# Dividing the activation's steps over a unit: three quarters with equal ScalarE work, and a transform step behind the copy out of X

## The chip, the core and the metric

The kernel runs on one core of a Trainium2 chip. The time is the device time of one execution in microseconds (us), from the first to the last instruction on that core. Before the change it is 2831.02 us, the median of three runs (2830.42 to 2831.22).

The engines have short names in the profile. PE is TensorE's matrix multiplication, and PEld is the loading of its stationary operand. DVE is VectorE, ACT is ScalarE and POOL is GpSimd. SP issues transfers. Each engine works through its own instructions strictly in the order in which they were written, so an instruction that waits holds up everything behind it on that engine.

## What is computed

The input x has 8 sequences of 3008 rows with 256 numbers each, in float32. A first part filters each sequence in the frequency domain; a second part is a two-layer network with an activation. Cut to what matters:

```
X = rfft(x, axis=1);  Y = X * (filt_r + 1j * filt_i);  a = irfft(Y, axis=1)
a = a.reshape(24064, 256)
h = a @ w_in                 # 24064 x 2048
out = (h - tanh(h)) @ w_out  # 24064 x 256
```

## The kernel before, in words

**The Fourier part** is three small dense transforms, with a round through device memory between each: `first` (64 points, tile pf), `middle` (47 points and back, with the filter in between; tiles pz on the way in and pe on the way out), and `last` (the return of the 64 points, tile pu). It is done for five groups of sequences. While the network works on one group, the transforms of the next are fed in between, one step at a time.

**The network part** treats up to 512 columns at a time (a "group" in the code; there are 48), and each group in four *units* U of 512 hidden features, so 192 units in all. A unit with its full width takes two by two blocks: instead of eight block products, it forms seven (a Strassen-Winograd scheme), both for w_in (function `up`) and for w_out (function `down`). GpSimd forms the sums of blocks (`combine`, lines 524 to 527).

Three generations of units are in work at once. While `up(U)` multiplies by w_in, `shrink(U-1)` applies the activation to the previous unit, and `down(U-2)` multiplies the one before that by w_out. Nothing plans this: `up` writes out by hand the order of everything, and calls the others through five small functions. `d()` and `e()` each advance `down` by one part (its matmuls, and at the end of a group the sums that follow them). `s()` advances `shrink` by one step, up to its next `yield`. `shrinks(k)` calls `s()` as often as the k-th number of the list `steps_at` says. `t(k)`, for k from 0 to 4, is a slot for the Fourier part: at most one step of `first`, `middle` or `last` is put there, if one is due, and some transfers of finished output. Its due times are spread evenly over a stretch of the kernel, so some stretches have a step in every slot, most have one in about every second slot, and the last 24 units have none but `last`.

**The four quarters of a unit.** The PSUM bank X takes four of `up`'s seven products one after the other: product 1, then 6, then 7, then 4. Between them X has to be read out: by ScalarE (`copied`, line 551: first into s1, then u2, then u3) and at last by VectorE (line 590, the third quarter of the tile h, called h2 below). The next product into X must wait for that copy, and the next unit's product 1 must wait for line 590. So X divides a unit into quarters, named here after their product: X1, X6, X7 and X4. The banks Y and Z take the other three products in between. TensorE's order before the change is: X1, Y, t(0), two products of `down`, t(1), X6, Z, two of `down`, t(2), X7, two of `down`, t(3), X4, one of `down`, t(4), Z, and then X1 of the next unit.

**The activation** works on the two halves of h (named 2 and 0 after where they begin). Each half passes ScalarE three times (arctan, line 611; square with a running sum, line 612; square with scale and bias, line 618) and VectorE twice (a product, line 617, which waits for line 612; a product with a sum, line 621, which waits for line 618). There are two buffers for y (lines 611, 612) and one for sq (line 618).

**The transform's steps** all use one PSUM buffer. A pz step has two matmuls (line 430), two ScalarE copies (lines 443, 444), a VectorE product that reads the same bank (line 445, tile uv) and two GpSimd operations (lines 446, 447). A pe step has two matmuls (line 411) and one ScalarE copy (line 414). A pf step is like a pe step. A pu step has eight short matmuls (line 511) and one copy (line 513). The next step's matmul can start only when the buffer has been read.

Of the kernel before, what the change touches and what calls it, by code (L numbers as in the profile page):

```python
# [143 lines left out]
def kernel(  # L144
# [10 lines left out]
    V, G, ACT = nc.vector, nc.gpsimd, nc.scalar  # L155
# [367 lines left out]
    def combine(b, t, shared=False):  # L523
        G.tensor_sub(t[0], b[0][1], b[0][0])  # L524
        G.tensor_sub(t[1], b[1][1], t[0])  # L525
        (V if shared else G).tensor_sub(t[2], b[1][1], b[0][1])  # L526
        G.tensor_sub(t[3], t[1], b[1][0])  # L527
# [4 lines left out]
    def up(U, d, e, s, t):  # L532

        i, u = divmod(U, 4)
        b, tu, w = uts[i]
        rhs = [b[0][0], b[1][0], b[1][1], tu[:, 3, 0:w], tu[:, 0, 0:w], tu[:, 1, 0:w],
               tu[:, 2, 0:w]]
        banks = {k: ps.tile([128, 2, 256], F32, tag=k, bufs=1, name=k) for k in "xyz"}
        X, Y, Z = (banks[k][:, :, 0:w] for k in "xyz")
        h = dn.tile([128, 4, 2, 256], F32, tag="h", bufs=3, name="h")  # L540
        hs[U] = (h, w)

        def mm(bank, q, first):
            for k in range(2):
                nc.tensor.matmul(bank[:, k], wu[:, q - 1, (2 * u + k) * 128:(2 * u + k + 1) * 128],  # L545
                                 rhs[q - 1], start=(first and k == 0), stop=True,
                                 skip_group_check=True)

        def copied(tag):
            t = dn.tile([128, 2, 256], F32, tag=tag, bufs=1, name=tag)[:, :, 0:w]  # L550
            ACT.copy(t, X)  # L551
            return t

        steps_at = ([1, 2, 0, 1, 0, 1, 1, 0] if U > 1 else [0, 0, 1, 0, 2, 0, 1, 2])

        def shrinks(at):
            for _ in range(steps_at[at]):  # L560
                s()

        mm(X, 1, True)
        mm(Y, 2, True)
        s1 = copied("s1")
        t(0)
        d()
        shrinks(0)
        V.tensor_add(h[:, 0, :, 0:w], Y, s1)  # L569
        e()  # L570
        shrinks(1)
        t(1)
        mm(X, 6, False)
        mm(Z, 5, True)
        u2 = copied("u2")
        shrinks(2)
        d()
        shrinks(3)
        e()
        t(2)  # L580
        mm(X, 7, False)
        u3 = copied("u3")
        V.tensor_add(h[:, 3, :, 0:w], Z, u3)  # L583
        shrinks(4)
        d()
        shrinks(5)
        e()
        t(3)
        mm(X, 4, False)
        V.tensor_copy(h[:, 2, :, 0:w], X)  # L590
        shrinks(6)
        d()
        e()
        t(4)
        mm(Z, 3, False)
        V.tensor_add(h[:, 1, :, 0:w], Z, u2)
        shrinks(7)

    def shrink(U):

        h, w = hs.pop(U)
        ht = {k: h[:, k:k + 2].rearrange("p a b n -> p (a b) n")[:, :, 0:w] for k in (0, 2)}

        def tiles(tag, bufs):
            return dn.tile([128, 4, 256], F32, tag=tag, bufs=bufs, name=tag)[:, :, 0:w]

        y, sq = {}, {}

        def start(k):
            y[k] = tiles("y", 2)  # L610
            ACT.activation(y[k], ht[k], AF.Arctan, scale=S)  # L611
            ACT.activation(y[k], y[k], AF.Square,  # L612
                           accum_out=y_sums[:, 2 * U + k // 2:2 * U + k // 2 + 1])

        def square(k):
            sq[k] = tiles("sq", 1)
            V.tensor_mul(ht[k], ht[k], y[k])  # L617
            ACT.activation(sq[k], y[k], AF.Square, bias=near_b, scale=A)  # L618

        def end(k):  # L620
            V.scalar_tensor_tensor(out=ht[k], in0=sq[k], scalar=K, in1=ht[k],  # L621
                                   op0=ALU.add, op1=ALU.mult)

        start(2)
        yield
        square(2)
        yield
        end(2)
        yield
        start(0)  # L630
        yield
        square(0)
        yield
        end(0)
        t = dn.tile([128, 4, 2, 256], F32, tag="t", bufs=2, name="t")
        blocks = [[h[:, 2 * a + k, :, 0:w] for k in range(2)] for a in range(2)]
        combine(blocks, [t[:, k, :, 0:w] for k in range(4)], U + 1 == 4 * len(groups))
        gs[U] = (blocks, t, w)
        yield
# [64 lines left out]
    def store(i, o):  # L704


        p, c = groups[i]
        r, n = CHUNKS[p][c]
        ws_ = widths(p, c)
        total = sum(ws_)  # L710
        ot = dn.tile([128, 2, CH * 128], F32, tag="ot", bufs=1, name="ot")
        for h in range(2):
            V.transpose(ot[:, h, 0:total], o[:, h, 0:total])
        b = UNITS[p][0]
        if len(UNITS[p]) == 2:
            blocks = [(r + 32 * q * NR, n, 32 * q) for q in range(4)]
        else:
            blocks = [(r_h + 32 * q * NR, n_h, rows.start + 32 * q)
                      for _, rows, r_h, n_h in halves(p, r, n) for q in range(2)]
        for h in range(2):  # L720
            for k in range(4):
                for row, m, lo in blocks:
                    outs.append((
                        dram(out.tensor, (b * SEQ + row) * DM + h * 128 + 32 * k,
                             [[NR * DM, 32], [DM, m], [1, 32]]),
                        ot[32 * k:32 * k + 32, h, :].rearrange(
                            "p (j c) -> p j c", c=128)[:, 0:m, lo:lo + 32]))
# [26 lines left out]
    def store_some(n):  # L754
        for dst, src in outs[:n]:
            nc.sync.dma_start(dst, src)
        del outs[:n]
# [81 lines left out]
    with tc.tile_pool(name="tr", bufs=2) as tr, tc.manual_schedule():  # L839
        with tc.tile_pool(name="pro", bufs=1) as pro, \  # L840
# [136 lines left out]
            for j in range(NK // 2):  # L977
# [7 lines left out]
                for i in range(2):  # L985
                    k = (2 * j + i) % 4
# [34 lines left out]
        with tc.tile_pool(name="dn", bufs=2) as dn, \  # L1021
# [40 lines left out]
            for U in range(total + 2):  # L1062
                i, u = divmod(U, 4)
                if U < total:
# [20 lines left out]
                    if u == 2 and i + 1 < len(groups):  # L1085
                        lasts = last(i + 1, z1)
                sh = shrink(U - 1) if 0 <= U - 1 < total else iter(())
                dw = down(U - 2) if 0 <= U - 2 < total else iter(())

                def d():  # L1090

                    next(dw, None)

                def e():

                    next(dw, None)

                def s():

                    next(sh, None)  # L1100

                def t(k):


                    nonlocal ms, done
                    if k == 2 and stores:
                        store(*stores.pop())
                    store_some(4)
                    if U >= total:
                        return  # L1110
                    pos = 20 * c + 5 * u + k
                    if u == 3 and k in (0, 2) and i + 1 < len(groups):
                        next(lasts)
                    elif done < len(steps) and steps[done] <= pos:
                        if done < n_f:
                            next(fs)
                        else:
                            next(ms)
                        done += 1
                        if done == n_f:  # L1120
                            ms = middle(p + 1, z1)
                            next(ms)
                    next(late, None)
                    if U > 0 and k in (1, 3):
                        next(copies, None)

                if U < total:
                    if U == total - 1:
                        one = tr.tile([128, 128], F32, tag="x", bufs=3, name="one_sb")
                        nc.sync.dma_start(one, one_d)  # L1130
                        ones = cst.tile([128, 1], F32, name="ones")
                        G.memset(ones, 1.0)
                    up(U, d, e, s, t)
                else:
                    for k in range(5):
                        s()
                        s()
                        d()
                        e()
                        t(k)  # L1140
                        if U == total + 1 and k == 0:
                            bounded(z1)
# [39 lines left out]
```

## Time and profile before

| what | before |
|---|---|
| time | 2831.02 us (2830.42 to 2831.22) |
| TensorE busy with matmuls | 2730.9 us, 96% of the span |
| VectorE busy | 1911.7 us, 68% |
| ScalarE busy | 1878.5 us, 66% |
| GpSimd busy | 1792.0 us, 63% |
| one full-width unit without a transform step | 12.09 us |
| matmul waits for the copy u2 or u3 (line 551) | 9.0 us in 24 waits |
| matmul waits for h2 (line 590) | 5.2 us in 9 waits |
| pe waits for uv (line 445) | 15.3 us in 23 waits |

The table of engines shows how long each was busy. A matmul's end is modelled, so its recorded time overlaps the next one's, and short stalls of TensorE are hidden under it. The waits of TensorE are therefore best read in two places: its matmuls (which show too little of a stall) and its weight loads (which show a little too much), and settled by the distance between the starts of two matmuls in the listing in order of time.

### The profile page before, as it was taken

To read this page: it belongs to the slowest core of one execution; us is meant where nothing else is said; L and a number is where in the kernel's file an instruction comes from. 1 tells how busy PE (TensorE), PEld (TensorE's weight loads), DVE (VectorE), ACT (ScalarE), POOL (GpSimd) and SP (SyncE) were. 2 spreads that over 40 slices of the span, in tenths; PEclk is the share of its full clock that TensorE was granted. 3 is DMA by queue.
4 is the path that set the end of the run, shared out by engine and by line. 5 is a ranking of instruction groups with operands and counts; after the bars stand their busy time and mean duration, and the time that the engine had idled before them with its cause. 6 is when DMAs were issued, how large, how long until landed. Compare 5 with 4: busy or idle time off the path is not lost.

```text
span 2831.1 us, 36652 instructions
## 1 busy us (share of the span) xinstructions
PE 2730.9 (96%) x12438; PEld 2269.8 (80%) x12438; DVE 1911.7 (68%) x2175; ACT 1878.5 (66%) x2790; POOL 1792.0 (63%) x1407
## 2 busy tenths in 40 slices
PE   4899999999999999999999999999999999999998
PEld 2577777988878777888877887788888888898887
DVE  6755556666766677666666777676676767677776
ACT  2466666666666677666677666666666676667665
POOL 5546777544777767644576777755466667655555
PEclk7999999999999999999999999999999999999999
DMA  9854443233233322222333223212222322101010
GB/s 249 217 179 118 104 116 76 71 94 85 59 81 85 77 67 54 57 81 81 85 81 74 70 66 86 49 40 68 58 65 62 79 56 53 34 18 26 16 22 17
DMA packets 322592, 217.53 MB, mean 77 GB/s; under 512 B 224782, under 2 KB 274746, under 8 KB 322156
## 3 DMA queue, kind: packets, MB, share of 16 engines
q1 hardware_dynamic: 266826, 157.28, 23.6%
q10 hardware_dynamic: 52818, 51.53, 6.0%
q0 software_dynamic: 2752, 6.30, 0.8%
q8 instruction: 100, 1.64, 0.2%
q14 instruction: 96, 0.79, 0.1%
HBM read 138.87 MB, written 79.17 MB: 77 GB/s over the span
## 4 chain that ended last, share of the span: by engine, by line
PE 78%; ACT 9%; issue 5%; DVE 5%; DMA 2%; POOL 1%; ACTq 1%; SPq 0%; DVEq 0%; POOLq 0%
PE o L663 31%; PE x L545 20%; PE z L545 9%; PE y L545 6%; PE pe L411 3%; PE pu L511 3%; ACT y L611 3%; PE pz L430 3%; PE pf L351 2%; DVE h L617 1%; ACT u L551 1%; ACT zs L444 1%; DVE uv L445 1%; ACT y L612 1%; ACT zs L443 1%
## 5 line engine op out<-in xcount | busy, mean ns | idle before, releaser
L663 PE MATMUL o<-t,wd 128*128 128x256 f32 (+2 forms) x3072 | 776.3, 375 | 1.8 <-POOL t L526 1.3
L617 DVE TENSOR_TENSOR h<-h,y 128x1024 f32<-128x1024 f32 (+2 forms) x384 | 571.3, 1488 | 275.8 <-ACT y L612 275.8
L663 PEld LDWEIGHTS o<-t,wd 128*128 128x128 f32 x3072 | 580.7, 190 | 74.2 <-POOL t L526 1.6
L545 PE MATMUL x<-tu,wu 128*128 128x256 f32 (+2 forms) x2304 | 588.0, 377 | 9.2 <-ACT u L551 9.0
L663 PE MATMUL o<-h,wd 128*128 128x256 f32 (+2 forms) x2304 | 582.5, 375 | 0.4 <-DVE h L621 0.4
L621 DVE SCALAR_TENSOR_TENSOR h<-sq,h 128x1024 f32<-128x1024 f32 (+2 forms) x384 | 568.0, 1479 | 20.6 <-ACT y L611 0.5
L524 POOL TENSOR_TENSOR t<-h 128x512 f32<-128x512 f32 (+2 forms) x192 | 240.4, 1252 | 506.8 <-DVE h L621 455.0
L545 PEld LDWEIGHTS x<-tu,wu 128*128 128x128 f32 x2304 | 427.4, 190 | 151.8 <-issue 72.6
L663 PEld LDWEIGHTS o<-h,wd 128*128 128x128 f32 x2304 | 431.1, 190 | 71.8 <-issue 18.4
L618 ACT ACTIVATE sq<-y,near_b 128x1024 f32<-128x1024 f32 (+2 forms) x384 | 435.6, 1134 | 5.0 <-DVE h L621 0.2
L611 ACT ACTIVATE y<-h 128x1024 f32<-128x1024 f32 (+2 forms) x384 | 400.0, 1042 | 15.7 <-ACT e L414 8.0
L612 ACT ACTIVATE y<-y 128x1024 f32<-128x1024 f32 (+2 forms) x384 | 399.2, 1040 | 12.2
L551 ACT COPY s<-x 128x512 f32<-128x512 f32 (+2 forms) x192 | 110.8, 577 | 441.0 <-PE x L545 432.4
L527 POOL TENSOR_TENSOR t<-t,h 128x512 f32<-128x512 f32 (+2 forms) x192 | 308.9, 1609 | 0.1
L551 ACT COPY u<-x 128x512 f32<-128x512 f32 (+2 forms) x384 | 219.2, 571 | 56.9 <-PE x L545 22.2
L583 DVE TENSOR_TENSOR h<-z,u 128x512 f32<-128x512 f32 (+2 forms) x192 | 129.5, 675 | 180.0 <-ACT u L551 177.0
L525 POOL TENSOR_TENSOR t<-h,t 128x512 f32<-128x512 f32 (+2 forms) x192 | 240.9, 1255 | 15.1
L526 POOL TENSOR_TENSOR t<-h 128x512 f32<-128x512 f32 (+2 forms) x191 | 248.0, 1298 | 0.0
L446 POOL TENSOR_TENSOR zs<-zs,ft 128x512 f32<-128x512 f32 x112 | 165.4, 1477 | 101.8 <-ACT zs L444 101.6
L447 POOL TENSOR_TENSOR uv<-uv,zs 128x512 f32<-128x512 f32 x112 | 213.7, 1908 | 15.7 <-DVE uv L445 7.2
L545 PE MATMUL x<-ut,wu 128*128 128x256 f32 (+2 forms) x768 | 199.2, 382 | 6.9 <-DVE h L590 5.2
L569 DVE TENSOR_TENSOR h<-y,s 128x512 f32<-128x512 f32 (+2 forms) x192 | 130.4, 679 | 104.9 <-PE y L545 88.6
(122 smaller groups left out, 3380.2 us busy)
## 6 DMA issues: line engine op xcount, KB each, us to landing
a<-ct SPq DMA_DIRECT2D x64, 384.0 KB, 4.1
ft<-filt SPq DMA_DIRECT2D x96, 256.0 KB, 4.6
out_dram<-ot SPq DMA_DIRECT2D x1392, 16.0 KB, 1.5
ct<-e ACTq DMA_DIRECT2D x112, 192.0 KB, 2.4
ct<-a ACTq DMA_DIRECT2D x80, 256.0 KB, 2.9
x_sb<-in_x_dram SPq DMA_DIRECT2D x69, 256.0 KB, 2.8
e<-ct SPq DMA_DIRECT2D x33, 512.0 KB, 4.7
fg<-fg SPq DMA_DIRECT2D x40, 392.0 KB, 6.0
```

Source lines behind the costliest of these rows:

```text
L524: G.tensor_sub(t[0], b[0][1], b[0][0])
L525: G.tensor_sub(t[1], b[1][1], t[0])
L526: (V if shared else G).tensor_sub(t[2], b[1][1], b[0][1])
L527: G.tensor_sub(t[3], t[1], b[1][0])
L545: nc.tensor.matmul(bank[:, k], wu[:, q - 1, (2 * u + k) * 128:(2 * u + k + 1) * 128], rhs[q - 1], start=(first and k == 0), stop=True, ski ...
L551: ACT.copy(t, X)
L611: ACT.activation(y[k], ht[k], AF.Arctan, scale=S)
L612: ACT.activation(y[k], y[k], AF.Square, accum_out=y_sums[:, 2 * U + k // 2:2 * U + k // 2 + 1])
L617: V.tensor_mul(ht[k], ht[k], y[k])
L618: ACT.activation(sq[k], y[k], AF.Square, bias=near_b, scale=A)
L621: V.scalar_tensor_tensor(out=ht[k], in0=sq[k], scalar=K, in1=ht[k], op0=ALU.add, op1=ALU.mult)
L663: nc.tensor.matmul(product(q), wd[:, q - 1, (2 * u + k) * 128: (2 * u + k + 1) * 128], rhs[q - 1][:, k], start=(u == 0 and k == 0 and q == ...
```

## The change

There are three edits.

1. The step of `shrink` that did a half's arctan and its square with sum is cut in two (`turn`, `power`), and the VectorE product is cut off from the last square (`times`, `square`). ScalarE still does the same six operations in the same order, and VectorE its four, but the `yield`s fall elsewhere. With the new list `steps_at`, ScalarE gets two of them in each of the quarters X1, X6 and X7: arctan and square with sum of half 2 in X1, the last square of half 2 and the arctan of half 0 in X6, and the square with sum and the last square of half 0 in X7. Before, it was three, two and one.
2. VectorE's line 621 for half 2 moves from X1, ahead of slot t(1), to X6, ahead of t(2).
3. The slot t(3) moves behind X4 and behind the copy out of X (line 590). Before, it stood ahead of both.

```
-        steps_at = ([1, 2, 0, 1, 0, 1, 1, 0] if U > 1 else [0, 0, 1, 0, 2, 0, 1, 2])
+        steps_at = ([1, 1, 1, 1, 0, 1, 1, 0] if U > 1 else [0, 0, 1, 0, 2, 0, 2, 1])
...
         shrinks(5)
         e()
-        t(3)
         mm(X, 4, False)
         V.tensor_copy(h[:, 2, :, 0:w], X)
+        t(3)
         shrinks(6)
...
-        def start(k):
+        def turn(k):
             y[k] = tiles("y", 2)
             ACT.activation(y[k], ht[k], AF.Arctan, scale=S)
+
+        def power(k):
             ACT.activation(y[k], y[k], AF.Square,
                            accum_out=y_sums[:, 2 * U + k // 2:2 * U + k // 2 + 1])
 
+        def times(k):
+            V.tensor_mul(ht[k], ht[k], y[k])
+
         def square(k):
             sq[k] = tiles("sq", 1)
-            V.tensor_mul(ht[k], ht[k], y[k])
             ACT.activation(sq[k], y[k], AF.Square, bias=near_b, scale=A)
...
-        start(2)
+
+        turn(2)
+        power(2)
+        yield
+        times(2)
         yield
         square(2)
+        turn(0)
         yield
         end(2)
         yield
-        start(0)
-        yield
+        power(0)
+        times(0)
         square(0)
         yield
         end(0)
```

## The prediction

> **What bounds the kernel now.** I read the page's table of engines first, then TensorE's waits, those of its weight loads, and last the listing in order of time.
>
> ```profile
> PE 2730.9 (96%) x12438; PEld 2269.8 (80%) x12438; DVE 1911.7 (68%) x2175; ACT 1878.5 (66%) x2790; POOL 1792.0 (63%) x1407
> ```
> ```profile
> 1000.00:1500.00 500.00, 496.13 (x2277) 412.35 (x2276) 334.50 (x370) 342.96 (x513) 311.02 (x236) 1.00 0.28 72
> ```
>
> TensorE is the bound, at a granted clock of 1.00; the change takes no matmul away. So it can win only TensorE's stalls, or add to them. These are the waits that the moved steps touch:
>
> ```profile
> PE pe L411 <- DVE uv L445: 15.3, 23, 2.7
> PE x L545 <- ACT u L551: 9.0, 24, 0.9
> PE x L545 <- DVE h L590: 5.2, 9, 1.8
> ```
> ```profile
> PEld x L545 <- ACT u L551: 29.2, 66, 1.1
> PEld x L545 <- DVE h L590: 22.9, 46, 2.2
> ```
>
> The columns are total us, times and longest. A recorded 256-column matmul lasts 379 ns, but in a full stretch one starts every 216 ns, so the first view hides some 0.16 us of each stall, and the second overstates. I therefore went through the listing and took the distance between starts beyond that pace: **22 us** for X6, X7 and X4, **18 us** for X1, and 42 us for pe, of which 18 are the prologue (before 123 us), untouched. That leaves 24 us of pe, nearly all in units 8 to 21, where every slot holds a step. So some 64 us are in reach.
>
> Where they arise:
>
> ```profile
> 822.07 1.13 PE L545 MATMUL x<-tu,wu 128*128 128x256 f32 x4 [0.67 <-ACT u L551]
> ```
> ```profile
> 794.20 0.69 DVE L445 TENSOR_TENSOR uv<-pz,ft 128x512 f32<-128x512 f32 x1 [1.30 <-ACT zs L444]
> 794.81 0.68 DVE L590 COPY h<-x 128x512 f32<-128x512 f32 x1
> ...
> 795.55 1.13 PE L545 MATMUL x<-ut,wu 128*128 128x256 f32 x4 [0.40 <-DVE h L590]
> ```
> ```profile
> 338.76 1.23 DVE L621 SCALAR_TENSOR_TENSOR h<-sq,h 128x1024 f32<-128x1024 f32 x1
> ...
> 339.90 0.68 DVE L445 TENSOR_TENSOR uv<-pz,ft 128x512 f32<-128x512 f32 x1
> ...
> 340.73 1.07 PE L411 MATMUL pe<-uv,fg 112*96 112x512 f32 x2 [1.54 <-DVE uv L445]
> ```
>
> First, X4 waits because u3 comes late from a busy ScalarE. Second, h2 (line 590) stands in VectorE's queue behind the uv of t(3), which waits for both ScalarE copies, and X1 waits for h2. Third, uv of t(1) stands behind line 621, and pe in t(2) waits for uv.
>
> [...] line 617 takes 937 ns at least, 1380 in the median and 2354 at most. This matters below. [...]
>
> **The change, part by part.** Times are us from the start of X1 in a full-width unit. From the listing I take these intervals: a product of `up` or `down` is 0.86 of TensorE (four matmuls of 0.216), a pz or pe step 0.87. A copy out of X can start 1.06 after its product starts; the next product into X can start 0.64 after the copy does. On ScalarE one thing follows another after 0.47 (copy), 1.09 (arctan), 1.18 (square with its sum read) and 1.06 (last square); the pair of zs copies takes 1.20 and starts at least 1.12 after pz. None of these change, since no operation does.
>
> *Relief of X6 and X7 (edit 1).* ScalarE in X1: before, s1 at 1.06, then arctan, square, last square: free at 4.86. After: 3.80. Take a unit of 820 us, with pe in t(0), pz in t(2), pe in t(4), the first of its kind in a group of four, in which `down` adds two ScalarE copies of 0.36. Before, its u3 started at 11.42 and X4 at 12.06; its slot was 11.23. After, pe's copy ends ScalarE's wait at 3.43, arctan and square take it to 5.70, p1 to 6.06, u2 to 6.55, last square and arctan to 8.70, p5 to 9.05, the zs copies to 10.26. So u3 starts at 10.26 and X4 may start at 10.90, before 11.23: the stall is gone. Where t(1) holds pz, u2 was at 7.50 and X7 waited to 8.13 for a slot of 7.77; after, u2 starts at 5.77. Moving t(3) brings X4 forward by 0.87 where t(3) has a step, but u3 then comes at 8.83 and X4 may start at 9.47, with its slot at 10.36. I take 18 of the 22 us: **−18**; between −10 (if u3 stays late where zs copies precede it) and −22.
>
> *h2 ahead of t(3) (edit 3).* h2 no longer waits for uv. Of the 18 us, 14 come from units with pz in t(3) or from unit 1, where line 621 stood in front; the rest are narrow groups and VectorE's own work. I take **−10**, between −6 and −14.
>
> *pe behind uv (edits 2 and 3).* In four dense units uv of t(1) stands no more behind line 621: 1.3 each, 2 in the last, −6. Six pe in t(3) get X4 as cover: 0.43 each, −2.6. But pz in t(3) and pe in t(4) are now one product apart (0.86) and not two (1.73), while uv comes 3 after pz: eight times +0.85, +6.8. Three pu behind uv gain 0.5 each, −1.5. Sum about **−3**, between −8 and +3.
>
> *The product of half 0 behind its square (edit 1; an added wait).* Before, line 617 of half 0 found its square long done and began as soon as h3 (line 583) was written. After, it waits for the square in X7, which starts 0.47 after u3: line 617 starts 0.47+1.18 = 1.65 after u3, and before 1.22. So +0.43. Behind it on VectorE stand `down`'s sums, and h2; for h2 waits X1.
>
> ```profile
> 2628.62 0.59 ACT L551 COPY u<-x 128x512 f32<-128x512 f32 x1
> ...
> 2629.84 1.22 DVE L617 TENSOR_TENSOR h<-h,y 128x1024 f32<-128x1024 f32 x1
> ...
> 2631.77 0.68 DVE L590 COPY h<-x 128x512 f32<-128x512 f32 x1
> ...
> 2632.73 1.03 PE L545 MATMUL x<-ut,wu 128*128 128x256 f32 x4
> ```
>
> Here h2 ends at 2632.45 and X1 needs it 0.05 before its start: the slack is 0.23, less than 0.43, so X1 loses 0.20. This is the second unit of a group. The first and fourth have 0.78 to spare; the third has 0.23, but its line 617 already starts 2.0 after u3, behind the output transposes, so it loses nothing. A step in t(3) or t(4) gives another 0.87. So about 20 units pay 0.2: +4. If pz is in t(2), the zs and uv operations of GpSimd are under way when line 617 now starts, [...] in about six units without cover +0.7: +4. Sum **+8**. From below 0, if h2 always has slack; from above 0.43 in 100 units, +43.
>
> *Line 621 of half 0 behind uv of t(3) (edit 3; an added wait).* It ends some 2.1 after the next X1, and `down`'s first product stands at 1.73: +0.4, unless t(0) has a step. About five units: **+2**. Between 0 and +10.
>
> *At nothing:* line 621 of half 2 in X6 (it was held until there by line 617 and GpSimd in the listing); the single sq buffer (read by 8.6, needed at 9.6); transfers; the epilogue, where the order on each engine is unchanged.
>
> Sum: −18 −10 −3 +8 +2 = −21: **2810 us**.
>
> **The rivals.**
> - *The stalls trade places, no change.* X4's relief is real, but line 617 reaches h2 late in every unit with a pz near it: +25 for that term and not +8. 2831 −21 +17 = **2827**; with a little less relief, **2830**. For it speaks that VectorE has only 0.23 to spare in half of the plain units; against it, that steps in t(3) and t(4) now both stand between X4 and X1.
> - *Slower.* [...] 48 second units pay 0.2 (+10), 40 units 0.9 (+36), `down` waits +5, relief −35 at most of which dense units give back 6: +22, **2853**. For it speaks the 2354 ns of line 617; against it, that GpSimd is done with `combine` by about 6.5 of a unit, and only pz in t(2) puts it under line 617.
> - *All of it.* 22 + 14 of the X waits and 10 of pe go, with 4 added: −42, **2789**. Against it: the 0.86 between t(3) and t(4).
>
> **How the numbers follow.** The forecast gets 0.68, no change 0.12, slower 0.12, all of it 0.08. The forecast's own terms run from about −33 to −8. The range 2800 to 2832 takes in the forecast and the trade, and leaves out most of the slower case and the large gain. Faster by over 0.2% (below 2825.4): 0.68 + 0.08 + 0.02 of the second = 0.78; within 0.2%: 0.10; slower: 0.12.
>
> **What would show it.** TensorE's waits for line 551 should fall from 9.0 to under 3 us, and the weight loads' from 29.2 to under 12; those for line 590 should remain, in second units and where pz is in t(2). The wait of line 617 for line 612 should rise. Waits of pe for uv should stay near 15 us, but sit in t(4). Units 168 to 191 should be slower by 1 to 2 us together, 24 to 119 faster by about 15. I am wrong if the waits for line 590 rise above 25 us in the weight loads' view with added time to match, or if u3 still comes late.

## The result, and the profile after

The changed kernel takes **2822.53 us** (2819.88 to 2824.63), the kernel before 2831.12 us (2829.45 to 2832.79), six runs each. The ratio is 0.9968, with a 95% interval of 0.9955 to 0.9981. So it is 8.6 us faster. Direction and range of the prediction hold; its size, 21 us, does not.

The page's table of engines of the changed kernel, and the stretch from 1000 to 1500 us (sum; busy time of PE, PEld, DVE, ACT and POOL with their instructions; granted clock; share and GB/s of the transfers):

```profile
PE 2727.4 (97%) x12438; PEld 2274.8 (81%) x12438; DVE 1915.9 (68%) x2175; ACT 1888.0 (67%) x2790; POOL 1769.1 (63%) x1407
```
```profile
1000.00:1500.00 500.00, 496.26 (x2292) 415.93 (x2291) 338.61 (x372) 346.59 (x516) 307.86 (x238) 1.00 0.29 71
```

The same 12438 matmuls, and in this stretch the same granted clock (1.00); 15 more of them fall into these 500 us than before (2292 against 2277), and yet PE's busy time in the stretch grew by 0.13 us only: busy time does not show this change. The waits do. Those of TensorE's matmuls in the changed kernel, where h2 is now line 589 and the half's second product line 625:

```profile
PE pe L411 <- DVE uv L445: 15.2, 16, 1.3
PE x L545 <- DVE h L589: 7.8, 18, 0.9
PE o L672 <- DVE h L625: 3.8, 8, 1.6
PE x L545 <- ACT u L551: 3.7, 4, 2.0
```

And those of its weight loads:

```profile
PEld x L545 <- DVE h L589: 24.3, 42, 1.3
PEld o L672 <- DVE h L625: 10.9, 20, 2.4
PEld x L545 <- ACT u L551: 6.0, 7, 2.4
```

The wait for u2 and u3 fell from 29.2 to 6.0 us in the second view. The wait for h2 did not fall, though edit 3 was meant to shorten it, and a wait of `down` for line 625 is new. VectorE's own waits name the cause: line 618 (the former 617) waits longer for its square. First before, then after:

```profile
DVE h L617 <- ACT y L612: 275.8, 144, 4.2
```
```profile
DVE h L618 <- ACT y L614: 313.1, 284, 5.8
```

Since neither view gives a stall its true size, I took from each kernel's listing the distance between the starts of neighbouring matmuls beyond their pace in a full stretch, by the product that came late. The table is for units 3 to 190; the last column is the time from the start of unit 3 to that of unit 191. The experiments are in it too.

| us | X6, X7, X4 | X1 | pe | pu | `down`'s first product | units 3 to 190 |
|---|---|---|---|---|---|---|
| before | 20.9 | 15.2 | 24.3 | 3.0 | 0.5 | 2630.1 |
| **after** | 4.2 | 18.7 | 24.8 | 0.8 | 4.3 | 2619.0 |
| slot alone | 27.0 | 7.5 | 28.9 | 3.0 | 4.3 | 2638.3 |
| steps alone | 2.4 | 29.5 | 20.0 | 0.8 | 0.9 | 2619.4 |
| square in X6 | 25.9 | 12.8 | 22.0 | 0.8 | 4.3 | 2632.1 |
| both early | 2.2 | 18.6 | 19.4 | 0.8 | 3.9 | 2610.1 |
| end first | 2.4 | 19.2 | 21.8 | 0.8 | 0.5 | 2610.5 |
| sums last | 2.4 | 15.5 | 20.1 | 0.8 | 4.1 | 2609.5 |
| all three | 2.4 | 13.3 | 21.8 | 0.8 | 0.9 | 2604.9 |
| no GpSimd filter | 2.4 | 9.9 | 15.0 | 0.8 | 0.5 | 2593.8 |

Before against after: −16.7 for X6, X7 and X4, +3.5 for X1, −1.7 for pe and pu together, +3.8 for `down`. That is −11.1, and units 3 to 190 are shorter by 11.1. Outside them the changed kernel loses 1.8 (1.65 after the start of unit 191), which leaves −9.3; the two profiled executions differ by 9.3.

Two places in the listing of the changed kernel show how the new wait works. The first is unit 173, a second unit with no step near:

```profile
2565.86 0.59 ACT L551 COPY u<-x 128x512 f32<-128x512 f32 x1 [0.49 <-PE x L545]
...
2567.52 1.23 DVE L618 TENSOR_TENSOR h<-h,y 128x1024 f32<-128x1024 f32 x1 [0.35 <-ACT y L614]
...
2569.46 0.68 DVE L589 COPY h<-x 128x512 f32<-128x512 f32 x1
...
2570.19 1.13 PE L545 MATMUL x<-ut,wu 128*128 128x256 f32 x4
```

Line 618 starts 1.66 after u3, where 1.65 was forecast. X1 comes 0.22 late by that, and its second matmul starts 0.32 after its first instead of 0.216: another 0.11. Together 0.33, where the forecast had 0.20. The second is unit 44, which has pz in t(2):

```profile
804.25 0.59 ACT L551 COPY u<-x 128x512 f32<-128x512 f32 x1
...
805.75 1.27 POOL L447 TENSOR_TENSOR uv<-uv,zs 128x512 f32<-128x512 f32 x1
805.92 2.19 DVE L618 TENSOR_TENSOR h<-h,y 128x1024 f32<-128x1024 f32 x1 [0.18 <-ACT y L614]
808.03 0.68 DVE L589 COPY h<-x 128x512 f32<-128x512 f32 x1
...
808.76 1.13 PE L545 MATMUL x<-ut,wu 128*128 128x256 f32 x4 [0.63 <-DVE h L589]
```

GpSimd's last operation of the step began 0.17 before line 618, which took 2.19 and not 1.23; h2 and X1 stood behind it. (In 189 of the units, in either trace, VectorE ran the eight instructions of `up` and `shrink` in the written order.) In this unit X4 no longer waits (0.55 before), and X1 behind it loses 0.90: the gain at X4 was given back at X1.

### The profile page after: what moved, and what is told of

It is laid out like the page before. It is cut to its first block, busy times and chain, and to the rows that moved or that the text cites. A ratio compares the mean times of both kernels' runs of the same rounds, so it can differ in the third digit from the quotient of the medians.

```text
span 2821.7 us, 36473 instructions
## 1 busy us (share of the span) xinstructions
PE 2727.4 (97%) x12438; PEld 2274.8 (81%) x12438; DVE 1915.9 (68%) x2175; ACT 1888.0 (67%) x2790; POOL 1769.1 (63%) x1407
## 4 chain that ended last, share of the span: by engine, by line
PE 82%; DVE 6%; ACT 4%; POOL 2%; issue 2%; DMA 2%; ACTq 0%; DVEq 0%; SPq 0%; POOLq 0%
PE o L672 34%; PE x L545 21%; PE z L545 10%; PE y L545 5%; PE pe L411 3%; PE pz L430 3%; PE pu L511 3%; DVE h L618 2%; PE pf L351 2%; ACT y L614 1%; DVE h L589 1%; DMA raw<-in_moe_w_in_dram 1%; ACT y L611 1%; DMA filt<-in_filt_r_dram 1%; DVE uv L445 1%
## 5 line engine op out<-in xcount | busy, mean ns | idle before, releaser
L618 DVE TENSOR_TENSOR h<-h,y 128x1024 f32<-128x1024 f32 (+2 forms) x384 | 578.8, 1507 | 314.5 <-ACT y L614 313.1
L625 DVE SCALAR_TENSOR_TENSOR h<-sq,h 128x1024 f32<-128x1024 f32 (+2 forms) x384 | 559.0, 1456 | 117.7 <-ACT sq L622 109.7
L527 POOL TENSOR_TENSOR t<-t,h 128x512 f32<-128x512 f32 (+2 forms) x192 | 319.1, 1662 | 0.1
L447 POOL TENSOR_TENSOR uv<-uv,zs 128x512 f32<-128x512 f32 x112 | 207.4, 1852 | 9.1 <-DVE uv L445 0.5
L545 PE MATMUL z<-tu,wu 128*128 128x256 f32 (+2 forms) x768 | 194.6, 376 | 0.0
```

## The experiments

**Which edit brings the gain?** Two kernels do a part each. Theory A is the sum by parts: edits 1 and 2 bring the relief and pay most of it back at X1, and the slot's move (edit 3) lowers the wait of X1 but raises that of pe. Rival B: the slot's move brings the gain. Rival C: edits 1 and 2 bring twice the gain, and the slot's move costs.

The slot alone is the kernel before with

```
-        t(3)
         mm(X, 4, False)
         V.tensor_copy(h[:, 2, :, 0:w], X)
+        t(3)
```

> The kernel before with edit 3 alone: slot t(3) behind X4 and the copy into h2, the steps of shrink as they were. Theory A (the relief of X4 by edit 1 came nearly in full, and the added waits were under-sized): without the relief, u3 is as late as before while X4 comes 0.87 us earlier in every unit with a step in t(3), so the stalls of X6, X7 and X4 grow from 22 us to about 28; X1's waits for h2 fall from 18 to about 9; pe in t(4) adds about 5. Sum +2: about 2833 us, no better than before. Theory B (edit 3 is what gained, edit 1 gave nothing): about 2822 us, as with both. Theory C (edit 3 eats a part of edit 1's relief): about 2836 us.

Measured: 2839.30 us, ratio 1.0026 (1.0016 to 1.0037). It is **slower**. X1 loses its wait as expected (15.2 to 7.5), but X6, X7 and X4 wait longer, pe by 4.6 longer, and `down` by 3.8. Its waits of TensorE:

```profile
PE pe L411 <- DVE uv L445: 21.0, 18, 2.8
...
PE x L545 <- ACT u L551: 13.0, 28, 2.0
```

X4 loses the cover of a step in t(3) while u3 is as late as before. B falls: alone, the slot's move does harm. The stalls of X and pe are those of theory A, but `down`'s were not in it, and the time is beyond A's number and C's. Another 1.3 us of it lies in unit 8, though its pe waits as long as before (2.9).

The steps alone are the changed kernel with t(3) back ahead of X4.

> The changed kernel with slot t(3) put back ahead of X4 (edits 1 and 2 alone). Theory A: the stalls of X6, X7 and X4 fall from 22 to about 5 us, pe in t(2) gains 2 to 3, X1's waits rise from 18 to about 25, since h2 still stands behind uv of t(3) and the product of half 0 now comes 0.43 later: about 2820 us, close to the whole change. Theory B: about 2831 us, no change. Theory C: about 2812 us, faster than the whole change by 10.

Measured: 2822.46 us, ratio 0.9968 (0.9955 to 0.998), the same time as the whole change. The relief is all here (X6, X7, X4 at 2.4), and so is the whole price of it: X1 waits 29.5, nearly twice as long as before.

```profile
PE x L545 <- DVE h L590: 13.6, 40, 0.9
...
PE pe L411 <- DVE uv L445: 10.2, 16, 0.8
```

So C falls too. By the table, the slot's move on top of the steps takes 10.8 from X1 and gives it back: 4.8 at pe, 3.4 at `down`, 1.8 at X6, X7 and X4. Edit 3 adds nothing to the steps, though its gain is as large as forecast.

**Is the relief to be had without the new wait?** If the square with sum of half 0 goes back to quarter X6, line 618 should find it done. The changed kernel with

```
         square(2)
         turn(0)
+        power(0)
         yield
         end(2)
         yield
-        power(0)
         times(0)
```

> The changed kernel with the square with sum of half 0 moved from quarter X7 back to X6 (edit 1's added wait taken away; ScalarE has three operations in X6 and one in X7). Theory A: line 618 of half 0 starts 1.22 us after u3 again, X1's waits for h2 fall from 19 to about 10 us; but u3 is later in units with a transform step in t(2), so the stalls of X6, X7 and X4 rise from 8 to about 14. Sum about -3: 2819 us. Rival: [...] X1's waits stay at 17 or more, and the time rises to about 2828 us by the stalls of X4.

Measured: 2834.11 us, ratio 1.0009 (1.0001 to 1.0018). X1's wait fell to 12.8, near what was expected, but X6, X7 and X4 wait 25.9: the relief is gone. My estimate of that side (8 to 14) was wrong. The relief and the new wait hang on one and the same square, which either stands ahead of u3 on ScalarE or behind it. With ScalarE's six operations in this order they come only together.

**Is it the distance of two neighbouring slots that eats edit 3?** With t(3) behind X4, a pz in t(3) and a pe in t(4) have one product between them. This kernel leaves t(3) ahead of X4 where t(3) and t(4) both hold a step, and behind X4 elsewhere:

```
+        early = both()
+        if early:
+            t(3)
         mm(X, 4, False)
         V.tensor_copy(h[:, 2, :, 0:w], X)
-        t(3)
+        if not early:
+            t(3)
...
+ def both():
+     pos = 20 * c + 5 * u + 3
+     return (done + 1 < len(steps) and steps[done] <= pos
+             and steps[done + 1] <= pos + 1)
```

> The changed kernel, but in a unit in which both t(3) and t(4) hold a step, t(3) goes ahead of X4 as it did before the change; in all other units behind the copy as in the change. Theory A (two steps one product apart hold each other up): pe's stall in t(4) goes back from 1.50 to 0.64 us in eight units (-7), pe in t(3) loses 0.43 in six (+2.6), and unit 4, whose copy waited for a transfer, gains 1.5: about -6, 2817 us, with units 9 to 19 together faster by about 4. Rival (the dense stretch is limited by the transform chain itself, each step by the copies of the one before): units 8 to 21 take as long in sum as with the change, within 1 us, and the time stays at 2822.

Measured: **2812.72 us**, ratio 0.9936 (0.9923 to 0.995), 9.8 below the changed kernel, more than expected. Unit 13 of the changed kernel, where pz is in t(3) and pe in t(4):

```profile
348.33 1.02 PE L430 MATMUL pz<-a,fg 94*128 94x512 f32 x2
...
350.72 0.69 DVE L445 TENSOR_TENSOR uv<-pz,ft 128x512 f32<-128x512 f32 x1 [0.39 <-issue]
...
351.56 1.07 PE L411 MATMUL pe<-uv,fg 112*96 112x512 f32 x2 [1.34 <-DVE uv L445]
```

and the same unit of this kernel:

```profile
343.79 1.02 PE L430 MATMUL pz<-a,fg 94*128 94x512 f32 x2
...
346.48 0.69 DVE L445 TENSOR_TENSOR uv<-pz,ft 128x512 f32<-128x512 f32 x1 [0.42 <-POOL o L703]
...
347.31 1.07 PE L411 MATMUL pe<-uv,fg 112*96 112x512 f32 x2 [0.77 <-DVE uv L445]
```

The uv comes 0.3 later here, and pe waits less all the same, since X4 now stands between. Units 9 to 19 gain 4.0, as expected; units 67 and 115, with the same pair of steps, 0.68 each; the 43 units 24 to 66 change by 0.08 in sum. Unit 8 gains 1.4, though its pe waits as long as in the changed kernel (4.2). Another 1.5 comes from unit 4, where three pf steps shared two buffers, and in the changed kernel a ScalarE copy (and with it u2 and u3) waited for a transfer:

```profile
184.63 0.59 ACT L352 COPY a<-pf 128x512 f32<-128x512 f32 x1 [3.53 <-DMA ct<-a]
```

**Can the other two waits be taken out of the order?** On top of the last kernel, three more. *End first* puts line 625 of half 0 ahead of the uv of t(3):

```
         V.tensor_copy(h[:, 2, :, 0:w], X)
+        shrinks(6)
         if not early:
             t(3)
-        shrinks(6)
```

> As e4_both_early, and in addition the last product of half 0 (line 625 of the change) ahead of slot t(3), so that it stands no more behind uv. Theory A: down's first product no longer waits where t(3) holds pz and t(0) nothing; its waits fall from 7.1 to about 4 us, and units 144, 146 and 148 lose their added 0.4 to 0.9 each. uv waits for ScalarE's copies at that point anyway, so pe loses nothing. About -3 beside e4_both_early: 2810 us. Rival: uv comes later by the 1.2 us of the product, and the next step's matmul waits that much longer; no gain, 2813 or more.

Measured: 2812.57 us, ratio 0.9933 (0.9919 to 0.9947); no gain over 2812.72. `down`'s wait went from 3.9 to 0.5, but pe's from 19.4 to 21.8, since uv now stands behind line 625. It is the rival's answer.

*Sums last* puts the VectorE sums of products 6 and 7, with which `down` ends a group in each second unit, behind h2 and line 625, so that h2 comes sooner there:

```
-        e()
...
         V.tensor_copy(h[:, 2, :, 0:w], X)
...
         shrinks(6)
+        e()
```

> As e4_both_early, but down's two VectorE sums at a group's end (in the second unit of each group) go behind h2 and behind line 625, out of the queue ahead of h2. Theory A (the start of line 618, 0.43 us later, is what holds X1 in the second units): the 0.22 us that units 169, 173, 177, 181, 185 and 189 hand on to the next go to zero, X1's waits fall from 19 to about 13 us, about -5 beside e4_both_early: 2808 us. Rival: X1 in those units waits for something else than VectorE's queue, the sums only move, and units 168 to 190 keep their +1.35.

Measured: 2811.25 us, ratio 0.9929 (0.9915 to 0.9942). X1's wait fell from 18.6 to 15.5, by 0.22 in a plain second unit, so VectorE's queue was the cause there, as theory A has it. But fourth units lose 0.10, and the third units 54, 66, 102, 114 and 146 gave back 0.7 to 0.86 each. The times of these last two kernels overlap with those of *both early*: singly, neither move has a gain clear of the spread.

*All three* has the order X4, copy, line 625, sums, t(3), with t(3) ahead of X4 where t(4) holds a step too.

> The moves of e4_both_early, e5_end_first and e6_sums_last together: t(3) ahead of X4 only where t(4) holds a step too, otherwise behind h2, line 625 and the sums. If the three waits are separate, as theory A has it, the gains add: -3 and -5 beside e4_both_early, about 2805 us. Rival: taking one wait away exposes the next on the same queue, and it stays within 2 us of the better of the two.

Measured: **2806.29 us** (2805.40 to 2808.89), ratio 0.9913 (0.99 to 0.9927). This version beats both kernels, by 25 and by 16 us. Together the two moves bring 6.4, where singly they brought 0.2 and 1.5. The waits are not additive: X1's is 13.3 here, below either move alone. The traces show where: units 54, 66, 102, 114 and 146, which together lose 3.8 with the sums last alone, gain 0.6 with both. That is 4.4 us of the difference between these two kernels; why the new place of t(3) mends these units, no run takes apart. What is left of the waits in question:

```profile
PE pe L411 <- DVE uv L445: 10.1, 16, 0.8
...
PE x L545 <- DVE h L591: 6.3, 14, 0.6
...
PE o L676 <- DVE h L629: 0.4, 1, 0.4
```

**How much of the added wait comes with GpSimd's operations?** If they are what makes line 618 take 2.19 and not 1.23 where pz is in t(2), it should take 1.23 there without them. The changed kernel without GpSimd's two operations of a pz step, in four of the five groups of sequences; it leaves out the cross terms of the filter:

```
-            G.tensor_mul(rows(zs), rows(zs), fi)
-            G.tensor_add(uv, uv, zs)
```

> The changed kernel with both GpSimd operations of the step pz left out in the stretch of four groups of sequences (lines 446 and 447), so the cross terms of the filter are left out. Theory A [...]: units 44, 45, 92, 93 and 156 lose X1's wait of 0.7 to 0.8, line 618 takes 1.22 instead of 2.1 in them, unit 8 gains about 3; about -8 beside the change: 2815 us. Rival (X1 waits there since line 618 starts late, for its square in X7): line 618 starts and X1 waits as before, within 2 us of 2822 but for unit 8.

Measured: 2797.23 us, ratio 0.988 (0.9865 to 0.9895), 25 below the changed kernel, where 7 to 8 were expected. The five units named in advance each lose about what was said: 0.79, 0.89, 0.82, 0.88 and 0.71. In unit 44 line 618 (here 616) takes 1.22 instead of 2.19:

```profile
803.36 0.59 ACT L549 COPY u<-x 128x512 f32<-128x512 f32 x1
...
803.83 1.22 DVE L616 TENSOR_TENSOR h<-h,y 128x1024 f32<-128x1024 f32 x1
```

X1's wait falls by 8.8, while that of second units stays at 7.3 us in 20 stalls (7.8 in 22). So about half of X1's 18.7 hangs on these two operations; in unit 44 line 618 is 0.97 shorter without them. The rest of the 25 was not in my theory: pe falls by 9.8 and `down` by 3.8. The wait of pe for GpSimd's part of uv (4.4 us in the changed kernel's matmuls) is gone, and unit 8 alone is 7.0 shorter; in the changed kernel TensorE stalls there for 4.35 us and then has a granted clock of 0.50 for 6.83 us (last section). This kernel bounds what GpSimd's part costs; it does not say what moving the two operations elsewhere would bring.

## Why the prediction was right in kind and too large

**Right.** The mechanism: ScalarE's relief lets u3 and so X4 come in time (−16.7 for −18), and it is paid with a later line 618. Three of the named signs came as said: pe's wait for uv stays near 15 (15.2) and sits in t(4), where units 11, 15 and 19 lose 0.86 each; the wait of line 618 for its square rises; units 168 to 190 lose 1.36, and unit 191 up to its last product 0.05. Two fell short. The waits for line 551 went to 3.7 and not below 3 (most of the rest is in units 0 to 2), though to 6.0 in the weight loads, below 12. And units 24 to 119 gained 11.0, not 15.

**What failed: the sizes, every one a little and to the same side.** The step of the prediction that failed most is "The product of half 0 behind its square". The wait is there, but it was put at +8. Since it was reckoned with the slot moved, it is measured by the change against the slot alone: **+11.2** at X1 (18.7 for 7.5), in 44 stalls for 22. It is 3.2 of a shortfall of 11.7, and the rest is spread over the other terms below. By kind of unit (with the one X1 after unit 190, so 0.1 to 0.3 more in all):

| X1's stalls, us (times) | slot alone | after | difference | forecast |
|---|---|---|---|---|
| second units | 2.8 (7) | 7.8 (22) | +5.0 | +4 |
| line 618 over 1.7 us (GpSimd) | 1.8 (4) | 7.0 (11) | +5.2 | +4 |
| third units | 1.9 (7) | 4.1 (10) | +2.2 | 0 |
| others | 1.1 (4) | 0.1 (1) | −1.0 | 0 |

Fifteen more second units stall and not 20, but each pays 0.33 and not 0.20, since the matmul after the late one comes 0.11 late as well; the 22 new stalls hold 2.4 us of that kind. Line 618 is stretched in more than the six units that I counted, and the +0.7 for each of them was my estimate. And third units were put at nothing because their line 617 already started 2.0 after u3; they do pay. Half of their loss is in 70, 118 and 166, of the narrow groups, where line 618 starts 0.37 later. Without the slot's move the same step costs +14.3 (steps alone against before).

By edit, the sum of the prediction put edits 1 and 2 at about −17 and edit 3 at about −4. Edits 1 and 2 alone brought 9.3, and edit 3 nothing on top of them.

The other terms:
- *h2 ahead of t(3)*, put at −10, brought 7.7 alone (10.8 on top of the steps). So X1 came to +3.5 in all, where −2 was forecast.
- *Line 621 of half 0 behind uv*, put at +2: `down` waits 3.8 longer. Units 144, 146 and 148 lose 0.47, 0.91 and 0.47 by it. Both *end first* and *no GpSimd filter* take the wait to 0.5, so it needs the new order and the GpSimd operations together.
- *pe behind uv*, put at −3 with pu: −1.7. In a dense unit pe in t(2) gained 0.77 and not 1.3; the 0.86 between t(3) and t(4) was right. Unit 21 gained 4.06 where 2 was forecast, and unit 8 lost 2.75; in both TensorE's half pace has a share. In unit 21 the granted clock is at 0.50 for 3.41 us before and not at all after, in unit 8 for 3.41 before and 6.83 after (last section).
- *Relief*: 1.3 short of its 18.
- *The end*, put at nothing, cost 1.65. Nearly all of it is TensorE's clock: after the last product of unit 191 the changed kernel runs two stretches of 3.41 us at a granted clock of 0.50 (from 2800.42 and from 2807.24 us) while it still has matmuls, the kernel before one (from 2815.88).

Together: 5.5 (X1) + 1.8 (`down`) + 1.3 (pe, pu) + 1.3 (relief) + 1.8 (outside units 3 to 190) = 11.7, and −21 + 11.7 = −9.3. No term of the sum held TensorE's half pace. By the distances of the matmuls in the stretches at 0.50 it cost some 1.6 at the end and 1.4 in unit 8, and gave 1.7 in unit 21: about 1.3 of the 11.7, an estimate.

Two figures of the prediction mislead. The 937 ns of line 617 are those of the narrow groups; at full width (128x1024) it takes 1198 ns at least and 1442 in the median. And the ends of its terms add up to −44 and +40, not to −33 and −8; how these two came about is not said.

**Of the rivals**, "the stalls trade places" came nearer in its number (2827 to 2830, 4.5 to 7.5 above the measured time; the forecast lay 12.5 below), but not by its mechanism: it had +25 for the term that measured +11. What remains open is how far the sizes by unit hold for other executions: each kernel has one trace.

## What to carry to other kernels

A step that is moved to balance one engine also moves the start of all that reads its result: price relief and new wait as one trade, unit by unit, with every instruction queued behind the one that waits. When a slot moves, look first at the slot after it: where two neighbours share a buffer or feed each other, the distance between them may be worth more than the gain (here, the choice by neighbour alone brought almost 10 us, 1.4 of them in unit 8, where pe waits as long). And repair the order as a whole: two moves that singly brought 0.2 and 1.5 us, no more than the spread, brought 6.4 together.

## What the runs showed of the hardware

**After its longest stalls TensorE ran at half its pace.** In unit 8 of the changed kernel, pe waited 4.18 us; the eleven matmuls after it start 427 ns apart and not 216. Four of them take 1.91 instead of 1.03:

```profile
245.48 1.23 DVE L618 TENSOR_TENSOR h<-h,y 128x1024 f32<-128x1024 f32 x1 [0.97 <-ACT y L614]
245.54 2.28 POOL L447 TENSOR_TENSOR uv<-uv,zs 128x512 f32<-128x512 f32 x1
...
247.88 2.02 PE L411 MATMUL pe<-uv,fg 112*96 112x512 f32 x2 [4.18 <-POOL uv L447]
249.69 1.91 PE L545 MATMUL x<-tu,wu 128*128 128x256 f32 x4
```

The granted clock is 0.50 from 247.25 to 254.07 us, for 6.83 us. A stall of 2.83 us (unit 21 before) was followed by slow matmuls too, seven of them 0.37 to 0.43 us apart, with the clock at 0.50 for 3.41 us. In the changed kernel that stall was 0.42, none was slow, and the unit gained 4.06 where the wait alone was 2.4.

The length of a stall did not decide by itself whether the half pace came. All stalls here are counted from start to start of the matmuls, beyond their pace. Unit 8 stalls for 3.03 us before, with 3.41 us at 0.50, and for 4.35 in the changed kernel, with 6.83. But at the end of the changed kernel two stalls of 1.45 and 0.70 us, from 2796.77 to 2800.35 us, came with 3.41 us at 0.50, and a single one of 2.16 us, from 140.17 to 142.55 us, with none. In each of these two traces, of the kernel before and the changed one, the stretches at 0.50 start whole multiples of 3.413 us apart. I divided both from 125 us on into pieces of that length on this grid, and took TensorE as occupied from each matmul's start to the next, but for no longer than its pace. At full clock, all 8 pieces that were occupied for at most 0.37 of their length were followed by one at half clock, and none of the 1564 occupied for 0.43 or more. The two short stalls at the end lie in one piece, occupied for 0.35 of it; the one of 2.16 lies across two. So in these two kernels short stalls counted together, and it mattered where on the grid a stall lay.

**Of line 618 and GpSimd's line 447, the one that started second took longer.** In the lines above, line 618 started 0.06 ahead of line 447, which then took 2.28. In the kernel before it was the other way round:

```profile
244.07 1.26 POOL L447 TENSOR_TENSOR uv<-uv,zs 128x512 f32<-128x512 f32 x1
...
244.31 2.11 DVE L617 TENSOR_TENSOR h<-h,y 128x1024 f32<-128x1024 f32 x1 [0.97 <-ACT y L612]
```

In the two traces, line 617 or 618 at full width started while line 447 was under way 52 times, and took 1.22 to 2.30, 2.10 in the median. Seven times it started 0.04 to 0.07 ahead of line 447: it took 1.20 to 1.23, and line 447 took 2.26 to 2.32. With none of GpSimd's additions and products beside it, it took 1.20 to 1.23 in all 234 cases. In unit 8 the changed kernel's order cost pe 1.3 us more (4.18 for 2.87). The rest of unit 8's 2.75 is TensorE's half pace, which the kernel before had there too, but for 3.41 us and not 6.83.
